# Attention block beside a gated MLP on one Trainium2 core: a planner's priorities and costs fitted anew, and one bias row spread over the partitions by GpSimd

## The chip, the core and the metric

The kernel runs on one core of a Trainium2 chip. The metric is the device time of one execution in microseconds (us): the median of three runs before the change is 158.12 us (158.08 to 158.12). Every view quoted here comes from one further execution under the hardware profiler. It took 157.98 us, of which the profile spans 156.2 us; the other 1.78 us lie outside the span. Engines are named PE (TensorE), DVE (VectorE), ACT (ScalarE), POOL (GpSimd) and SP (SyncE, which here only issues DMAs). A name with a q behind it (POOLq, SPq) is that engine's instruction queue, its sequencer.

## The reference

```python
x = A_x                                   # 1 x 2048 x 448, bf16
xn = _layernorm(x)
# A: 16 heads of 28; a token sees 8 keys, at 0, 2, ... 14 tokens back
qkv = xn @ wqkv;  kg, vg = k[idx], v[idx]
logits = einsum("bhsd,bhswd->bhsw", q, kg) * 28**-0.5   # masked where idx < 0
s = einsum("bhsw,bhswd->bhsd", softmax(logits), vg) @ wo
# B: a two-layer MLP, 448 -> 1792 -> 448
g = silu(gelu(xn @ w1 + b1) @ w2 + b2)
return x + s * g
```

## The kernel before

**The tiling.** The 2048 tokens are 16 tiles of 128 partitions, four tiles to a chunk. Even and odd tokens are laid in separate halves, so that keys 2 apart become neighbours. A tile is normalised (`stats`, `rstds`, `norm`: lines 400 to 444), turned to xnT (by PE for tiles 0 to 3, by SP's transposing DMA, L360, for the others), projected to q, k (L532) and v (L556), and q and k are turned by L360 again. The first MLP layer (`ff1`, L591, gelu on ACT at L595) goes by chunk, the second (`ff2`, L627, then y, tanh and g at L649, L655, L659) by tile.

**Attention** goes in nine visits of 228 (once 224) tokens: scores (L677, 64 matmuls), exp (ACT, L687), mask (L693, DVE or POOL), the weighted sum over v (L709, 64 matmuls), and the division through two DVE transposes (L719 to L733). POOL copies the windows of v by DMA (`move_v`, L354). `final` (L796 to L811) multiplies by wo, forms sg and o and stores the tile.

**What orders the work.** Nothing is scheduled by hand. Each piece of work is a task with an engine, a cost in us, dependencies, pool buffers and a priority. `_Plan.run` (L89) walks through time with these costs: on each engine the task that can start first goes next, and among those within `SLACK` of it the one of highest priority. The result is a fixed program order on each engine. So a cost or priority changes no operation; it changes the order on every queue.

**Pairs and hops.** Most projections and all of `ff1` have a contraction of 448 = 3 x 128 + 64. `pair` (L477) splits two such products into 64-row matmuls that run side by side on the two halves of the PE array: a first part of 8 matmuls, then a second part of 6 with the halves swapped. Between the two stands a hop: an instruction that waits for the first part and tells PE that it is done (L490). Its queue is POOL for the chunks 0 and 1 (`early`), SP or POOL later:

```python
held["told"] = (nc.gpsimd if k.on == "POOL" else nc.sync).nop()
...
told = plan.add(HOPS[0] if early else HOPS[1], 0.06, f2, [t], 300)
...
u = plan.add("PE", pe(a.n, 3), f3, [told], prio + LATER["swap"], ...)
```

**rstd on POOL.** For tiles 4 and up, 1/sqrt(var + eps) is formed on POOL in two instructions, the second waiting for the first:

```python
nc.gpsimd.tensor_scalar(sd[:, t0:t0 + n], ...)                                          # L425
nc.gpsimd.tensor_tensor(out=rstd[:, t0:t0 + n], in0=sd[...], in1=half_t, op=ALU.pow)    # L426
```

**b2** (L894) is loaded before by one DMA, issued by POOL, that reads the row of 448 numbers 128 times, once for each partition (112 KB). y (L649) and the last tile (L625) need it.

Of the kernel before, what the change touches and what calls it, by code (L numbers as in the profile page):

```python
# [164 lines left out]
def kernel(  # L165
# [12 lines left out]
    nc = tc.nc  # L178
    P = 128
    S, D, H, DH, F = A_x.shape[1], 448, 16, 28, 1792  # L180
# [9 lines left out]
    TPC = CH // P  # L190
# [26 lines left out]
    def sb(name, shape, dt=BF16):  # L217
        return const.tile(shape, dt, name=name)
# [11 lines left out]
    b2 = sb("b2", [P, D])  # L230
# [15 lines left out]
    def ring(name, n, shape, dt=BF16, fifo=False):  # L246
        return _Pool([sb(f"{name}{i}", shape, dt) for i in range(n)], fifo)
# [10 lines left out]
    p_o = ring("o", 3, [P, D])  # L258
# [9 lines left out]


    PRIO = {  # L270
        "project": (49.5, 205, 104, 52.5,),
        "project2": (147, 150, 101, 61,),
        "values": (89.5, 62.5, 21, 58,),
        "attn": (185, 179.5, 78, 174.5, 106.5, 106, 138.5, 136.5, 32.5,),
        "ff1": (185, 180, 84.5, 176.5, 66.5, 64.5, 156.5, 189.5, 203, 146, 76, 114.5, 77.5, 179.5,
            75.5, 118.5, 180.5, 14.5, 163, 68, 151, 115.5, 194.5, 167.5, 180, 188.5, 86, 93,),
        "gelu": (62.5, 22.5, 95, 92.5,),
        "ff2": (144, 162.5, 103.5, 142.5, 44.5, 112.5, 67, 5, 89, 106.5, 101.5, 75, 74, 55, 11.5,
            6.5,),
        "final": (140, 19.5, 70.5, 47, 112, 34.5, 23.5, 142.5, 73, 53, 198.5, 188.5, 81.5, 126.5,  # L280
            180, 71,),
        "norm": (37.5, 132, 179.5, 129.5, 74.5, 99, 161, 69, 63, 62, 43.5, 73, -5.5, 90, 133.5,
            150,),
        "loads": (166.5, 166, 188, 139.5, 54.5,),
        "stats": (47.5, -60, 180.5, 23, 127, 56, 188.5, 77, 197.5, -13.5, 185, 205.5, 138, 14, 52.5,
            138.5,),
        "turn_x": (108.5, -1, 28, 116, 210, 116.5, 131.5, 160, 41.5, 79.5, 70, 119, -4.5, 74.5,
            132.5, 111,),
        "turn_qk": (68.5, 112, 174.5, 90, 80, 6, 149.5, 60.5, 4, 140.5, 199.5, 96.5, 103, 166.5,
            140, 156,),  # L290
        "move_v": (81.5, 95, 23, 95, 18.5, 26.5, 8, 128, 29.5,),
        "copies": (50, 119.5, 58.5, 76, 32.5, 135.5, 43, 1, 87, 79.5, 129, 77, 32, 41.5, 135,),
    }
    LATER = {"swap": 135, "qk": 165, "v": 29.5, "gelu": 30.5, "exp": 55.5, "mask": -60, "pv": 45, "recip": -16.5, "os": 54.5, "y": 153.5, "tanh": 182.5, "g": 58, "sg": 183, "o": 120.5}

    plan = _Plan()

# [3 lines left out]
    def pe(n, k=1):  # L301
        return k * (n / 2400.0 + 0.0025)

    def act(n):
        return 0.15 + n / 1130.0
# [39 lines left out]
    def dma(eng, dst, src, kb, prio, deps=(), issue=0.5, rate=350.0):  # L345
        def fn(_):
            {"SP": nc.sync, "ACT": nc.scalar, "POOL": nc.gpsimd}[eng].dma_start(dst, src)
        a = plan.add(eng, issue, fn, [t_on] + list(deps), prio)
        return plan.add("DMA", kb / rate, lambda _: None, [a], prio, tail=1.7)
# [123 lines left out]
    def behind(later, earlier):  # L473
        tc.add_manual_dep(later.ins, earlier.ins.name,
                          mybir.DependencyInfo(mybir.DependencyClass.Sync, mybir.DependencyReason.DATA), reason="row tiles")

    def pair(a, b, prio, early=False):  # L477
# [17 lines left out]
        def f3(k):  # L495
            p, q = buf(p_b, t, 0), buf(p_b, t, 1)
            for i in together([part(b, q, kt, 0, kt + 4) for kt in range(3)], [part(a, p, kt, 1, kt + 4) for kt in range(3)])[0]:
                behind(i, held["told"])
        u = plan.add("PE", pe(a.n, 3), f3, [told], prio + LATER["swap"], tail=0.15, mode=64)
        a.evac(u, t, 0)  # L500
# [23 lines left out]
    t_row, t_qk = [[] for _ in range(NT)], {}  # L524

    def qk_rows(t, which, prio):
        cs = slice(t * P, (t + 1) * P)

        def part(ps, kt, half, start, stop):
            r = half_rows(half)  # L530
            w = w_in[r, kt, which * D:(which + 1) * D] if kt < 3 else w_in3[r, 0, :]
            return nc.tensor.matmul(ps[:, :D], xnT[r, kt, cs], w, start=start, stop=stop)  # L532

        def evac(a, own, i):
            b = qk_tok[t % len(qk_tok)]

            def fn(k):
                copy(k.on, b[:, which, :, :DH], buf(p_b, own, i)[:, :D].rearrange("p (h c) -> p h c", h=H))
            t_row[t].append(plan.add(("ACT", "DVE"), (act(D), dve(D)), fn, [a, t_qz[t % len(qk_tok)], t_qk.get(t - len(qk_tok))],
                                     prio + LATER["qk"], give=((p_b, own, i),)))  # L540
            if len(t_row[t]) == 2:
                t_qk[t] = dma_T(qkT[:, :, :, cs].rearrange("p w g c -> p (w g) c"), lambda: b[:].rearrange("p w h c -> p (w h c)"),
                                t_row[t], PRIO["turn_qk"][t], None, 2, 1.9 if t < 3 else 3.8 if t == TPC else 2.0 if t == TPC + 1 else 1.27)
        return _Job(D, part, [t_xT[t]] + t_w[0] + t_w[1] + t_w[2], evac, (), t_w[3])

    t_v, v_at, h_at = {}, {}, {}
# [3 lines left out]
    def vproj(t, prio):  # L550
# [7 lines left out]
        def evac(a, own, i):  # L558
            def fn(k):
                copy(k.on, v_tok[t][:, :, :DH], buf(p_b, own, i)[:, :D].rearrange("p (h c) -> p h c", h=H))  # L560
            t_vt[t] = plan.add(("ACT", "DVE"), (act(D), dve(D)), fn, [a] + t_vw + v_used[t], prio + LATER["v"], give=((p_b, own, i),))
        return _Job(D, part, [t_xT[t]] + t_w[0] + t_w[1] + t_w[2], evac, (), t_w[3])
# [22 lines left out]
    def ff1(c, mt, prio, gate):  # L585
# [7 lines left out]
        def evac(a, own, i):  # L593
            def fn(k):
                nc.scalar.activation(buf(p_h, own, i)[:], buf(p_b, own, i)[:], ACT.Gelu_apprx_tanh,  # L595
                                     bias=b1[:, mt:mt + 1])
            t_h[(c, mt)] = plan.add("ACT", 0.69, fn, [a, t_b1] + gate, prio + LATER["gelu"],
                                    give=((p_b, own, i),), table=("gelu",))
# [17 lines left out]
    def ff2_part(t, cs, n, end, prio):  # L616
# [30 lines left out]
        else:  # L647
            def f2(k):
                nc.vector.tensor_tensor(out=buf(p_y, k)[:, :n], in0=buf(p_b, halves[0])[:, :n], in1=b2[:, cs], op=ALU.add)  # L649
            y, pool = plan.add("DVE", dve(n), f2, [a, t_b2], prio + LATER["y"], take=(p_y,), give=((p_b, halves[0], 0),)), p_y  # L650
            held = ((p_y, y, 0),)
        after = [a, y]

        def f3(k):
            nc.scalar.activation(buf(p_t, k)[:, :n], buf(pool, y)[:, :n], ACT.Tanh, scale=0.5)  # L655
        th = plan.add("ACT", act(n), f3, after, prio + LATER["tanh"], take=(p_t,), table=("exp", "gelu"))

# [85 lines left out]
    def attn(b, what):  # L743

        deps, take, give, fns, cost = [], [], (), [], -SWITCH
        for n, (w, blk) in enumerate(what):
            if not n or what[n - 1][0] != w:
                cost += SWITCH
            cost += 0.215
            if not n:  # L750
                cost += 0.03
            at = len(take)
            if w == "S":
                fn, d = scores_of(blk)
                d = d + state["early"]
                take += [p_b] * 4
                fns.append(lambda k, fn=fn, at=at: fn([buf(p_b, k, at + i) for i in range(4)]))
            else:
                exps, masked = state[blk]
                fn, g = values_of(blk, exps)  # L760
                give += g
                d = masked + t_v[blk]
                take += [p_b] * 2
                fns.append(lambda k, fn=fn, at=at: fn([buf(p_b, k, at + i) for i in range(2)]))
            deps = deps + d + last_visit[w][-1:]

        def f1(k):
            for fn in fns:
                fn(k)
        prio = PRIO["attn"][b]  # L770
        a = plan.add("PE", cost, f1, deps, prio + (LATER["pv"] if what[0][0] == "P" else 0), take=take, give=give, tail=0.15,
                     mode=32 if what[0][0] == "S" else 33)
        a.out = 32 if what[-1][0] == "S" else 33
        at, exps = 0, []
        for w, blk in what:
            last_visit[w].append(a)
            if w == "S":
                state[blk] = weights_of(blk, a, at, PRIO["attn"][blk], state["gate"])
                exps += state[blk][0]
                at += 4  # L780
            else:
                for w in range(2):
                    output_of(blk, a, at + w, w, PRIO["attn"][blk])
                at += 2
        return exps
# [95 lines left out]
    def f_b1(k):  # L881
# [7 lines left out]
    turned = [t_xT[t].deps[0] for t in range(TPC, 2 * TPC)]  # L889
# [1 line left out]
    load_x(12, 4, 85, "SP", turned)  # L891
    t_w2 = [[dma("SP", w2[:, 7 * i:7 * i + 7, :], B_w2[F // 2 * i:F // 2 * (i + 1), :].rearrange("(m p) c -> p m c", p=P),
                 784, PRIO["loads"][4], turned, 1.0)] for i in range(2)]
    t_b2 = dma("POOL", b2[:], B_b2.rearrange("(o d) -> o d", o=1).to_broadcast((P, D)), 112, 82, turned)  # L894
    t_wo += [dma("POOL", wo[32 * g:32 * g + 28, :, :], A_wo[112 * g:112 * g + 112, :].rearrange("(l c) d -> c l d", l=4),
                 100, 80, [t_w2[1][0]] + t_wo[:1]) for g in range(G)]
    for t in range(2 * TPC, NT):
# [69 lines left out]
```

## Time and profile before

| | |
|---|---|
| median of 3 runs | 158.12 us |
| profiled execution, and its span | 157.98 us, 156.2 us |
| busy share of the span: PE, DVE, ACT, POOL | 96%, 72%, 53%, 48% |
| PE idle in the span | head 1.2 us, wait before L677 0.2 us, after the last matmul the rest |
| matmuls and weight loads | 2204 each |
| chain that ended last | PE 80%, DVE 8%, DMA 3%, POOL 2%, issue 2% |
| POOL: masks (L693), v copies (L354) | 28 (24 + 4), 52 |
| DVE: masks (L693) | 8 |

Section 1 of a page gives the busy time of each engine. Matmul ends are modelled, so a PE row that is "busy" can hide a wait; the starts of successive groups in the timeline show it. The chain of waits is followed back from the last instruction. A releaser is inferred: where it names an engine that had long been done, it was something else in the queue.

### The profile page before, as it was taken

To read this page: it belongs to the slowest core of one execution; us is meant where nothing else is said; L and a number is where in the kernel's file an instruction comes from. 1 tells how busy PE (TensorE), PEld (TensorE's weight loads), DVE (VectorE), ACT (ScalarE), POOL (GpSimd) and SP (SyncE) were. 2 spreads that over 40 slices of the span, in tenths; PEclk is the share of its full clock that TensorE was granted. 3 is DMA by queue.
4 is the path that set the end of the run, shared out by engine and by line. 5 is a ranking of instruction groups with operands and counts; after the bars stand their busy time and mean duration, and the time that the engine had idled before them with its cause. 6 is when DMAs were issued, how large, how long until landed. Compare 5 with 4: busy or idle time off the path is not lost.

```text
span 156.2 us, 5305 instructions
## 1 busy us (share of the span) xinstructions
PE 150.1 (96%) x2204; PEld 77.8 (50%) x2204; DVE 113.2 (72%) x259; ACT 83.3 (53%) x149; POOL 74.7 (48%) x123
## 2 busy tenths in 40 slices
PE   6999999999999999999999999999999999999980
PEld 2544454444455555455554644455556444545570
DVE  4789551486266758997799895109899996998992
ACT  3245867378889416444634149782496587051220
POOL 7854856000459408839261098389599780000000
PEclk9999999999999999999999999999999999999999
DMA  4999969999749443099039822123300100200211
GB/s 156 329 317 315 167 124 187 237 269 307 141 95 166 64 82 90 10 192 138 4 83 85 131 70 73 38 76 83 105 0 4 34 31 29 63 4 0 68 36 43
DMA packets 33575, 17.36 MB, mean 111 GB/s; under 512 B 25331, under 2 KB 32387, under 8 KB 33552
## 3 DMA queue, kind: packets, MB, share of 16 engines
q1 hardware_dynamic: 31472, 14.03, 41.3%
q0 software_dynamic: 1936, 2.88, 8.5%
q8 instruction: 17, 0.28, 0.8%
q10 hardware_dynamic: 144, 0.11, 0.2%
q14 instruction: 6, 0.05, 0.1%
HBM read 7.06 MB, written 1.84 MB: 57 GB/s over the span
## 4 chain that ended last, share of the span: by engine, by line
PE 80%; DVE 8%; DMA 3%; POOL 2%; issue 2%; ACT 1%; SPq 1%; DVEq 0%; ACTq 0%; POOLq 0%
PE bank L627 23%; PE bank L591 22%; PE bank L532 11%; PE bank L796 7%; PE bank L556 6%; PE bank L677 4%; PE bank L709 4%; PE bank L327 3%; DMA xnT<-xn 3%; POOL v L354 2%; DVE sg L801 2%; DVE o L807 1%; DVE w_in L659 1%; ACT E L687 1%; DVE xn L438 1%
## 5 line engine op out<-in xcount | busy, mean ns | idle before, releaser
L627 PE MATMUL bank<-w,h 128*128 128x448 bf16 (+1 forms) x238 | 45.2, 342 | 0.0
L591 PE MATMUL bank<-xnT,w 64*128 64x512 bf16 x392 | 44.7, 376 | 0.0
L595 ACT ACTIVATE h<-bank,b 128x512 bf16<-128x512 f32 x56 | 34.0, 689 | 12.9 <-PE bank L591 12.8
L354 POOL DMA_DIRECT2D v<-v_tok x52 | 27.6, 538 | 19.8 <-PE bank L709 9.0
L693 POOL TENSOR_TENSOR E<-E,m_gen 128x456 bf16<-128x456 bf16 x24 | 26.7, 1139 | 11.7 <-ACT E L687 9.5
L627 PEld LDWEIGHTS <-h 128*128 128x128 bf16 x238 | 22.3, 98 | 18.1 <-issue 0.4
L591 PEld LDWEIGHTS <-w 64*128 64x128 bf16 x392 | 19.1, 94 | 22.7 <-issue 1.1
L532 PE MATMUL bank<-w_in,xnT 64*128 64x448 bf16 (+1 forms) x212 | 24.3, 350 | 0.1
L687 ACT ACTIVATE E<-bank 128x456 bf16<-128x456 f32 (+1 forms) x36 | 17.0, 555 | 9.1 <-PE bank L677 9.1
L655 ACT ACTIVATE t<-y 128x448 f32<-128x448 f32 x15 | 8.7, 578 | 17.4 <-DVE y L649 17.4
L719 DVE STREAM_TRANSPOSE dt<-bank 128x480 f32<-128x480 f32 (+1 forms) x18 | 12.1, 671 | 5.6 <-PE bank L709 5.6
L532 PEld LDWEIGHTS <-xnT 64*128 64x128 bf16 (+1 forms) x212 | 10.6, 94 | 10.9 <-issue 1.1
L314 DVE CAST qk_tok<-bank 128x448 bf16<-128x448 f32 x16 | 9.4, 613 | 6.8 <-PE bank L532 6.8
L796 PE MATMUL bank<-wo,oT 128*128 128x448 bf16 (+1 forms) x68 | 14.1, 342 | 0.0
L312 ACT CAST qk_tok<-bank 128x448 bf16<-128x448 f32 x16 | 8.3, 533 | 10.6 <-PE bank L532 10.0
L556 PE MATMUL bank<-w_in,xnT 64*128 64x448 bf16 (+1 forms) x106 | 13.4, 349 | 0.0
L649 DVE TENSOR_TENSOR y<-bank,b 128x448 f32<-128x448 f32 x15 | 9.3, 620 | 4.9 <-PE bank L627 4.9
L728 DVE STREAM_TRANSPOSE dt<-rd 128x480 f32<-128x480 f32 (+1 forms) x18 | 12.1, 673 | 0.5
L733 DVE TENSOR_TENSOR oT<-bank,dt 128x456 bf16<-128x456 f32 (+1 forms) x18 | 11.3, 630 | 0.5
L404 DVE BATCH_NORM_STATS2 st<-x_sb 128x6 f32<-128x448 bf16 x16 | 9.6, 603 | 2.4 <-DMA x_sb<-in_A_x_dram 2.4
L438 DVE TENSOR_SCALAR xn<-x_sb,mv,rstd 128x448 bf16<-128x448 bf16 x16 | 6.3, 394 | 6.0 <-POOL rstd L426 5.8
L796 PEld LDWEIGHTS <-oT 128*128 128x128 bf16 x68 | 6.3, 98 | 6.3 <-issue 0.8
(62 smaller groups left out, 128.9 us busy)
## 6 DMA issues: line engine op xcount, KB each, us to landing
out_dram<-o SPq DMA_DIRECT2D x15, 112.0 KB, 1.7
w<-in_B_w_dram SPq DMA_DIRECT2D x2, 784.0 KB, 7.2
w<-in_B_w_dram SPq DMA_DIRECT2D x2, 672.0 KB, 7.0
x_sb<-in_A_x_dram SPq DMA_DIRECT2D x3, 448.0 KB, 6.3
v<-v_tok POOLq DMA_DIRECT2D x20, 64.0 KB, 2.5
w_in<-in_A_wqkv_dram SPq DMA_DIRECT2D x3, 336.0 KB, 4.3
w<-in_B_w_dram SPq DMA_DIRECT2D x4, 112.0 KB, 6.5
wo<-in_A_wo_dram POOLq DMA_DIRECT2D x4, 98.0 KB, 4.2
```

The lines of the kernel that those rows point to most:

```text
L354: nc.gpsimd.dma_start(dst(k), src())
L532: return nc.tensor.matmul(ps[:, :D], xnT[r, kt, cs], w, start=start, stop=stop)
L556: return nc.tensor.matmul(ps[:, :D], xnT[r, kt, k0:k0 + P], w, start=start, stop=stop)
L591: return nc.tensor.matmul(ps[:], w1[r, kt, ms], xnT[r, kt, cs], start=start, stop=stop)
L595: nc.scalar.activation(buf(p_h, own, i)[:], buf(p_b, own, i)[:], ACT.Gelu_apprx_tanh, bias=b1[:, mt:mt + 1])
L627: nc.tensor.matmul(ps[:, :n], buf(*h_at[(c, mt)])[:, j * P:(j + 1) * P], w2[:, mt, cs], start=(mt == 0 and not biased), stop=(mt == NMT - 1))
L687: nc.scalar.activation(buf(p_E, k)[:, :n], buf(p_b, a, at + hl)[:, :n], ACT.Exp, scale=SCALE)
L693: (nc.gpsimd if k.on == "POOL" else nc.vector).tensor_tensor(out=E[:, :n], in0=E[:, :n], in1=m[:, :n], op=ALU.mult)
L719: nc.vector.transpose(buf(p_dt, k)[:, :32 * m], buf(p_b, po, i)[:, :32 * m])
L728: nc.vector.transpose(buf(p_dt, d)[:, :32 * m].rearrange("p (b c) -> p b c", c=32), buf(p_rd, r)[:, :m].unsqueeze(2).to_broadcast((P, m, 32)))
L733: nc.vector.tensor_tensor(out=oT[:, :, q0:q0 + 2 * nq], in0=buf(p_b, po, i)[:, :n].rearrange("p (l q) -> p l q", l=4), in1=buf(p_dt, d)[:, ...
L796: nc.tensor.matmul(ps[:, :n], oT[:, kt, t * P:(t + 1) * P], wo[:, kt, cs], start=(kt == 0), stop=(kt == KT - 1))
```

## The change

Three things are changed, and no arithmetic:

- All priorities (`PRIO`, `LATER`) are replaced.
- Two costs of the planner are changed: an attention visit on PE from 0.215 to 0.47 us (to which the planner adds 0.095 for a switch of tiling and 0.03), and the issue of a qkT transpose on SP from 3.8, 2.0, 1.27 to 4.5, 2.2, 1.6 us for tiles 4, 5 and 6.
- b2 is loaded as one row into the last output buffer, and a new POOL instruction copies it to all partitions.

```diff
     PRIO = {
-        "project": (49.5, 205, 104, 52.5,),
+        "project": (76, 203, 109, 106.5,),
...
-    LATER = {"swap": 135, "qk": 165, "v": 29.5, "gelu": 30.5, "exp": 55.5, "mask": -60, "pv": 45, "recip": -16.5, "os": 54.5, "y": 153.5, "tanh": 182.5, "g": 58, "sg": 183, "o": 120.5}
+    LATER = {"swap": 182.5, "qk": 143.5, "v": 37.5, "gelu": 172.5, "exp": 90.5, "mask": 35, "pv": 53, "recip": 48, "os": 171, "y": 181, "tanh": 144, "g": 137, "sg": 134, "o": 74}
...
-                                t_row[t], PRIO["turn_qk"][t], None, 2, 1.9 if t < 3 else 3.8 if t == TPC else 2.0 if t == TPC + 1 else 1.27)
+                                t_row[t], PRIO["turn_qk"][t], None, 2, 1.9 if t < 3 else 4.5 if t == TPC else 2.2 if t == TPC + 1 else 1.6 if t == TPC + 2 else 1.27)
...
-            cost += 0.215
+            cost += 0.47
...
-    t_b2 = dma("POOL", b2[:], B_b2.rearrange("(o d) -> o d", o=1).to_broadcast((P, D)), 112, 82, turned)
+    b2r = p_o.bufs[-1]
+    t_b2r = dma("POOL", b2r[:1], B_b2.rearrange("(o d) -> o d", o=1), 1, 82, turned[:1])
+    t_b2 = plan.add("POOL", 0.5, lambda _: nc.gpsimd.partition_broadcast(b2[:], b2r[:1], channels=P), [t_b2r], 82)
```

The built program's order on each engine shows what the diff does not:

- The number of matmuls is the same, and so is the number of ACT table loads (6).
- On DVE there are 18 masks where there were 8, 13 o additions (L807) where there were 17, and 26 copies out of PSUM (L314) where there were 25. POOL has 18 masks where it had 28, and the other 4 o additions.
- POOL's order holds two further instructions. One, of the kind that stands at L335 ahead of the first affine_select (there the profile shows it as MODIFY_POOL_CONFIG), stands directly ahead of the new partition_broadcast and names another code library, number 1; a second stands ahead of the next L425, and names library 0 again.
- Between POOL's instructions the hops stand so (a hop is named by the number of the matmul that it waits for, counted through PE's order): 206, 214, then library 1 and the broadcast, 234, 242, 262, 270, 290, then library 0, L425, L426 (tiles 8 to 11), 298, 312, L425, L426 (tiles 12 to 15), 320, 340 and so on. Before, the order was 206, 214, 234 and so on up to 326, L425, L426, 346, L425, L426.
- PE's order in that stretch: matmuls 207 to 214 are a first part of `ff1`; 283 to 290 and 291 to 298 are first parts of v, 299 to 304 the second part that hop 290 lets go, 305 to 312 and 313 to 320 first parts of `ff1`, and 321 to 326 the second part that hop 298 lets go. Then come the rest of chunk 1's `ff1`, q and k of the tiles 8 and 9, and the first scores.
- On PE, q and k of the tiles 10 to 15 and v of the tiles 8 to 15 now stand together (84 matmuls of L532, 56 of L556). Between the first two score visits of the last chunk stand 18 matmuls of `ff2` and `final` (before: 14 of `ff2`), and the last visit's sum over v stands alone, ahead of the last 6 matmuls of `ff1`.
- On SP, four qkT transposes (before: three) stand ahead of the first xnT transpose of tile 4, and both halves of w2 are loaded ahead of the qkT transposes of tiles 4 to 7.

## The prediction

> **What bounds the kernel now.** I read the busy shares first, then PE's timeline, then the chain of waits, then what POOL's queue does around L425.
>
> ```profile
> PE 150.1 (96%) x2204; PEld 77.8 (50%) x2204; DVE 113.2 (72%) x259; ACT 83.3 (53%) x149; POOL 74.7 (48%) x123
> ```
>
> PE is the bound. Its columns in the next view are start, length, instruction, tiles, shape and count.
>
> ```profile
> 23.50 5.88 PE L532 MATMUL bank<-w_in,xnT 64*128 64x448 bf16 x56
> 29.21 13.11 PE L591 MATMUL bank<-xnT,w 64*128 64x512 bf16 x120
> 42.16 0.92 PE L556 MATMUL bank<-w_in,xnT 64*128 64x448 bf16 x8
> ...
> 61.68 5.47 PE L532 MATMUL bank<-w_in,xnT 64*128 64x448 bf16 x56
> 67.08 0.93 PE L796 MATMUL bank<-wo,oT 128*128 128x448 bf16 x4
> ...
> 114.14 0.40 PE L677 MATMUL bank<-qkT 32*64 32x57 bf16 x6
> 114.76 0.65 PE L677 MATMUL bank<-qkT 32*64 32x57 bf16 x58 [0.22 <-ACT E L687]
> 115.34 2.82 PE L627 MATMUL bank<-w,h 128*128 128x448 bf16 x14
> ...
> 150.75 0.93 PE L796 MATMUL bank<-wo,oT 128*128 128x224 bf16 x8
> ```
>
> From start to start, 120 matmuls of L591 take 42.16 - 29.21 = 12.95 us, 0.108 each; 56 of L532 take 67.08 - 61.68 = 5.40 us, 0.096 each. The same 56 take 5.71 at 23.50: 0.3 of hidden waiting, for xnT (the chain passes there from a DMA of xnT to PE at 27.31). The scores at 114.14 take 1.20 instead of the 0.63 of other visits: 0.57 of waiting. I find no other wait worth a name between 10.6 and 151.7. So an order can win only about 1 us inside PE's stretch and something in the tail, while whatever makes PE wait is lost in full. Hence the question is what PE waits for in the new order, and this leads to POOL: PE's second parts of pairs wait for hops in POOL's queue.
>
> **The change part by part.**
>
> *The order.* Counted through the built order:
> - The wait of 0.3 at 27.3: q and k of the tiles 6 and 7 are now behind 34 matmuls of `ff1` (3.7 us), so their xnT is there. But tile 4's first xnT transpose stands behind a fourth qkT transpose on SP (L360, 1.27 us) and can be up to 0.5 late. I take -0.1, between -0.3 and +0.4.
> - The wait of 0.57 at 114: between the two score visits there are now 18 matmuls of L627 and L796 (18 x 0.19 = 3.4 us) against 14 (2.75), and ACT needs 1.28 for its table and 4 x 0.47 for the exps, 3.2. I take -0.5, between -0.57 and 0.
> - The tail: the last matmul ends at 151.68, the last DVE instruction at 153.38, because DVE still divides the last visit (L723 to L733, 147.87 to 149.48) among the last finals. Now that visit's sum stands 6 matmuls of `ff1` and 28 of L627 earlier than the finals. I take -0.5, between -0.9 (DVE then only waits for PE) and 0.
> - Against this DVE has 10 more masks at 0.39, 4 fewer o additions at 0.39, one more copy at 0.61: +3.0 us on an engine that is idle 43 us. PE hides it, except in the last third, where DVE is nearly full. I take +0.2, between 0 and +1.
>
> Together -0.9 (between -1.8 and +1.4).
>
> *b2's DMA.* 112 KB fewer on queues that are not on the chain: 0.
>
> *The broadcast on POOL.* The copy itself is short: POOL's rows for one instruction on such a tile run from 0.2 (memset of 128 columns) to 1.05 (mask of 456); I take 0.5. The price is in the two instructions that the diff doesn't show, which name library 1 and then library 0. The only such instruction in the trace names library 0 at the start:
>
> ```profile
> L335 POOLq MODIFY_POOL_CONFIG  x2: 7/9/11, 0.9 to 1.0; - x2
> L335 POOL TENSOR_SCALAR_AFFINE_SELECT ident<-ident x1: 293/293/293, 1.1 to 1.1; 128x128 bf16<-128x128 bf16 x1
> ```
>
> Two writes of 9 ns, and 0.1 us later an affine_select of the ordinary 293 ns. That shows that naming a library that is there costs nothing. It does not show what fetching another costs. Bounds from rows: below, 0.13 us (0.94 to 1.07); above, a transfer of that stretch, since code has to come by DMA. The columns are transfers, KB each and us to landing; the first row is of the issues between 24 and 28 us alone, the second of the whole span.
>
> ```profile
> w<-in_B_w_dram SPq DMA_DIRECT2D x1, 784.0 KB, 8.6
> ```
>
> ```profile
> w<-in_B_w_dram SPq DMA_DIRECT2D x2, 784.0 KB, 7.2
> ```
>
> I take 8.6 for the first fetch, which starts beside that very load (27.02), and 7.2 for the second: the start row is for a library already there, the loads are rows of a stretch in which all DMA queues are full.
>
> The Trainium skill bears on this: "GPSIMD Engine Reference", section "Instruction dispatch", says that the first call to a freshly loaded POOL kernel pays about 6 us to bring its code in, with no instruction in the profile that shows it. No run here shows it yet. With 5.95 for each fetch the sum below would be 161.3 instead of 164.0; with the start row's 0.13 it would be 157.1.
>
> *When.* Matmul 214 ends at 23.50 + 44/56 x 5.71 = 28.0 now; in the new order 22 of the matmuls ahead are L591 instead of L532 (+0.3) and the wait of 0.3 is gone: 28.0. Behind it come 34 of L591 and 42 of L532/L556 up to matmul 290: 3.7 + 4.0, so 35.7. Matmuls 291 to 320 (14 and 16): 1.35 + 1.73, so PE reaches matmul 321 at 38.8 and needs hop 298 there.
>
> *Who is held.* Do hops pass while POOL works? The chain says so:
>
> ```profile
> 17.41 0.30 POOL sd L425
> ...
> 17.76 0.02 POOLq L490
> ...
> 17.80 0.73 POOL rstd L426
> ```
>
> This hop stands behind L426 in the queue, but passes at 17.76, when L425 has ended and L426 has just been handed over, not at 18.53, when L426 ends. So the queue runs ahead of the work and is held only by an instruction that itself waits: L426, for L425's result. In the new order the hops 234 to 290 are behind the broadcast, which waits for a small DMA alone, and pass. But hop 298 is behind L426, which waits for L425, which needs library 0. Before, L425 had its hops ahead of it and it was POOL that waited:
>
> ```profile
> POOL sd L425 <- PE bank L591: 14.5, 1, 14.5
> ```
>
> Sum: library 1 from 28.0 to 36.6, the broadcast to 37.1, library 0 to 44.3, L425 and its handover (0.4) to 44.7. PE has waited since 38.8: **5.9 us**. The hops 312 and 320 follow at once or 1.5 us later, when PE has 20 matmuls to do. The later chain of tiles 8 and 9 (rstd, xn, transposes) is late by as much as PE, so it adds nothing. Without the fetches L425 would run when the seventh statistic is there (some 37.5 by DVE's rows: loads landed at 31, 0.73 a tile, two copies) and hop 298 would be 0.9 ahead of PE.
>
> *PE's clock.* After the idle start the warm-up matmuls of 512 columns come one in 0.43 us, twice the 0.216 of a full pair later:
>
> ```profile
> 3.78 0.15 PEld L327 LDWEIGHTS <-h 128*128 128x128 bf16 x1 [0.28 <-issue]
> 4.21 0.15 PEld L327 LDWEIGHTS <-h 128*128 128x128 bf16 x1 [0.28 <-issue]
> ```
>
> This lasts from 1.25 to 5.06, 3.8 us at half rate, a loss of 1.9. Whether an idle stretch of 6 us brings it back is not in this trace: between 0 and 1.9, I take the middle, 1.0. The Trainium skill ("TensorE: Matmul & The Clock Gate", section "The HAM clock gate") has the clock halved after about 3.4 us of idleness and restored after as long of work; by that it would be 1.7, and the total 0.7 more.
>
> **Sum** on the profiled execution: 157.98 - 0.9 + 5.9 + 1.0 = 164.0 us. The median of the runs is 158.12, 0.14 above it; I leave that inside the rounding: **164.0 us**.
>
> **Rivals.**
>
> *The queue itself stands still while a library is fetched* (18%). For: the profile shows no such fetch, so my evidence on hops is of ordinary instructions only. Against: the two writes at the start ran while a memset was still at work. Then hop 234 comes at 36.6, while PE needs it 28 matmuls behind 214, at 31.0: 5.6; the second switch is reached at 41.3 and lets hop 298 go at 48.9, needed at 44.4: 4.5. With the clock twice: 157.98 - 0.9 + 10.1 + 2.0 = 169.2 us.
>
> *The way back is short, or no code is fetched at all* (16%): faster. Place: hop 298. It decides where the second switch takes less than 38.8 - 35.7 - 0.4 = 2.7 us; the first is hidden up to 7.2 in any case. For: the row at L335. Then only the order is left: 157.98 - 0.9 = 157.1 us. The change then does what it says.
>
> *The order alone goes wrong* (4%): the seventh statistic, the first xnT of tile 4, or a mask on the fuller DVE comes late, fetches cost nothing, 158.5 to 160.
>
> **How the numbers follow.** Forecast 62%: with fetches of 5 us each PE waits 2.3, with 8.6 each 7.3 and 1.9 of clock, with the order's bounds 159 to 168. The range must reach to the first rival and leaves out the faster one (16%) and the edges: 159 to 171 us. A measurement of this kernel can tell about 0.2%, 0.3 us, from no change. Faster 0.13 (most of the second rival), same 0.02, slower 0.85.
>
> **What would show it.** Right: after, two gaps of several us on POOL, one ahead of the broadcast and one ahead of the L425 at 36 to 45 us; PE with a wait ahead of the L556 group of 6 (matmul 321), released by POOL's queue; hops 234 to 290 on time. The stall at 114 gone, the DVE end closer to PE's. Wrong: PE dense from 28 to 45 us (no fetch, or a short one), or a first wait already ahead of the L591 group at 31 us (the queue stands still), or L425 late for want of statistics.

## The result, and the profile after

The changed kernel takes 170.06 us (median of four runs, 168.46 to 170.53), the kernel before 158.1 beside it: ratio 1.0746, interval 1.0671 to 1.082. It is slower by 7.5%. The profiled execution is the shortest of the four: 168.46 us, span 166.7, so 10.5 us of span more than before. In the changed kernel every line behind the table `PRIO` is one lower, up to the load of b2 (L555 is before's L556, L424 and L425 are before's L425 and L426, the hop is L489); the new broadcast is L895. The page's second part, a digit for each fortieth of the span:

```profile
PE   7999989994199999989989998999999899999990
PEclk9999999999569999999999999999999999999998
```

Before, PE's row was nines from the second slice to the 38th. A slice is now 4.17 us. PE falls to 4 and 1 tenths in the slices 10 and 11 (37.5 to 45.8 us), and the granted clock (PEclk) is down to 5 and 6 tenths in the slices 11 and 12. PE's timeline (start, length, instruction, count, idle time ahead and its releaser) says where the rest lies:

```profile
24.02 0.93 PE L531 MATMUL bank<-w_in,xnT 64*128 64x448 bf16 x8 [0.53 <-DMA xnT<-xn]
...
37.46 1.89 PE L590 MATMUL bank<-xnT,w 64*128 64x512 bf16 x16
45.26 1.30 PE L555 MATMUL bank<-w_in,xnT 64*128 64x448 bf16 x6 [5.91 <-POOLq L489]
46.35 7.30 PE L590 MATMUL bank<-xnT,w 64*128 64x512 bf16 x54
53.49 2.81 PE L531 MATMUL bank<-w_in,xnT 64*128 64x448 bf16 x28
...
71.60 2.81 PE L626 MATMUL bank<-w,h 128*128 128x448 bf16 x14 [0.62 <-DVE y L648]
...
84.96 4.70 PE L555 MATMUL bank<-w_in,xnT 64*128 64x448 bf16 x47 [0.44 <-DVE qk_tok L313]
...
104.42 0.93 PE L795 MATMUL bank<-wo,oT 128*128 128x448 bf16 x4 [0.96 <-DVE oT L732]
```

I measure a loss from start to start: the time to the next group's start, less the count times the rate at which the same matmuls go undisturbed (0.108 us for L590, 0.096 for the 64-row ones, 0.187 for L626). It comes out a little larger than the idle time in brackets (6.1 against 5.91 us ahead of L555). For the changed kernel's profiled execution this gives:

| where PE loses | us |
|---|---|
| ahead of L555, hop 298 | 6.1 |
| the 60 matmuls behind it, at the lower clock | 1.8 |
| tile 4's xnT, at 24 (before: 0.3 for xnT at 27) | 0.9 |
| VectorE late: y at 71, qk_tok at 79 and 85, oT at 104, sg and y at 132, the visit at 147 (before: none) | 0.7 + 0.4 + 0.7 + 1.1 + 0.8 + 0.4 = 4.1 |
| scores near 114 (before: 0.6) | 0 |
| last matmul to the end of the span: 3.9 (before 4.5) | -0.6 |

With before's own 0.3 and 0.6 taken off, that is 6.1 + 1.8 + 0.6 + 4.1 - 0.6 - 0.6 = 11.4; the remaining -0.9 lies in differences under 0.5 us each, some -0.3 of it in the first 16 us.

What held PE is told by POOL's rows (instruction, count, duration in ns, first and last start) for the two fetches, and by the chain of waits in order of time:

```profile
L895 POOLq MODIFY_POOL_CONFIG  x2: 16/16/16, 28.8 to 28.9; - x2
L895 POOL PARTITION_BROADCAST b<-o x1: 518/518/518, 37.3 to 37.3; - x1
```

```profile
L424 POOLq MODIFY_POOL_CONFIG  x2: 120/120/120, 37.8 to 37.8; - x2
```

```profile
38.53 6.32 issue
44.85 0.30 POOL sd L424
...
45.19 0.03 POOLq L489
...
45.26 1.30 PE bank L555 x6
```

The reader is to see a POOL that does nothing from 28.9 to 37.3 and from 37.9 to 44.85, with no instruction in the gaps. The hop passes when L424 ends, and PE starts 0.07 us later. During the first gap PE's timeline has no wait at all: the hops 234 to 290 passed. I call such a gap a fetch, after the instruction that names another library. What fills it the profile doesn't show: it has no instruction there, and in the kernel with the broadcast alone (below) no DMA traffic is recorded in the second gap (0 GB/s).

### The profile page after: what moved, and what is told of

Its sections match the earlier page's. It is cut to its first block, busy times and chain, and to the rows that moved or that the text cites. A ratio compares the mean times of both kernels' runs of the same rounds, so it can differ in the third digit from the quotient of the medians.

```text
span 166.7 us, 5308 instructions
## 1 busy us (share of the span) xinstructions
PE 152.0 (91%) x2204; PEld 79.0 (47%) x2204; DVE 118.0 (71%) x266; ACT 83.0 (50%) x148; POOL 68.4 (41%) x118
## 4 chain that ended last, share of the span: by engine, by line
PE 60%; DVE 19%; DMA 9%; issue 7%; SPq 2%; POOL 1%; ACT 1%; DVEq 0%; POOLq 0%; ACTq 0%
PE bank L626 19%; PE bank L590 17%; PE bank L531 8%; PE bank L795 6%; PE bank L555 5%; DMA x_sb<-in_A_x_dram 5%; DMA v<-v_tok 4%; DVE st L403 3%; PE bank L708 2%; DVE w_in L658 2%; PE bank L676 2%; DVE sg L800 2%; DVE y L648 2%; SPq L359 1%; DVE qk_tok L313 1%
## 5 line engine op out<-in xcount | busy, mean ns | idle before, releaser
L590 PE MATMUL bank<-xnT,w 64*128 64x512 bf16 x392 | 46.2, 384 | 0.0
L626 PE MATMUL bank<-w,h 128*128 128x448 bf16 (+1 forms) x238 | 45.4, 342 | 0.6 <-DVE y L648 0.6
L626 PEld LDWEIGHTS <-h 128*128 128x128 bf16 x238 | 22.4, 98 | 19.4 <-issue 1.8
L590 PEld LDWEIGHTS <-w 64*128 64x128 bf16 x392 | 19.6, 96 | 23.5 <-issue 3.1
L531 PE MATMUL bank<-w_in,xnT 64*128 64x448 bf16 (+1 forms) x212 | 24.7, 350 | 0.9 <-DMA xnT<-xn 0.5
L692 POOL TENSOR_TENSOR E<-E,m_gen 128x456 bf16<-128x456 bf16 x15 | 16.3, 1102 | 12.3 <-ACT E L686 10.5
L555 PE MATMUL bank<-w_in,xnT 64*128 64x448 bf16 (+1 forms) x106 | 13.6, 362 | 6.4 <-POOLq L489 5.9
L531 PEld LDWEIGHTS <-xnT 64*128 64x128 bf16 (+1 forms) x212 | 11.2, 94 | 11.4 <-issue 1.1
L437 DVE TENSOR_SCALAR xn<-x_sb,mv,rstd 128x448 bf16<-128x448 bf16 x16 | 6.3, 394 | 14.5 <-POOL rstd L425 10.7
L732 DVE TENSOR_TENSOR oT<-bank,dt 128x456 bf16<-128x456 f32 (+1 forms) x18 | 11.4, 632 | 0.6
L555 PEld LDWEIGHTS <-xnT 64*128 64x128 bf16 (+1 forms) x106 | 6.2, 96 | 11.7 <-POOLq L489 6.4
L311 ACT CAST v_tok<-bank 128x448 bf16<-128x448 f32 x8 | 4.3, 536 | 14.3 <-PE bank L555 14.2
```

What stands on the lines that cost most here:

```text
L311: nc.scalar.copy(o, i)
L555: return nc.tensor.matmul(ps[:, :D], xnT[r, kt, k0:k0 + P], w, start=start, stop=stop)
L590: return nc.tensor.matmul(ps[:], w1[r, kt, ms], xnT[r, kt, cs], start=start, stop=stop)
L626: nc.tensor.matmul(ps[:, :n], buf(*h_at[(c, mt)])[:, j * P:(j + 1) * P], w2[:, mt, cs], start=(mt == 0 and not biased), stop=(mt == NMT - 1))
L692: (nc.gpsimd if k.on == "POOL" else nc.vector).tensor_tensor(out=E[:, :n], in0=E[:, :n], in1=m[:, :n], op=ALU.mult)
```

## The experiments

My theory behind the result: two library fetches make rstd of tiles 8 to 11 late, PE stands still for it and loses clock, and besides that the new order is worse by itself. The rivals: the order's losses are only an echo of the stall; a fetch costs by itself, wherever it stands; the slow matmuls behind the stall are slow for another reason; the hop alone is what holds PE. Ratios are to the kernel before on the same chip. Every kernel computes the whole reference.

**The order without the broadcast.** The changed kernel's order, b2 by before's DMA:

```diff
-    t_b2r = dma("POOL", b2r[:1], B_b2.rearrange("(o d) -> o d", o=1), 1, 82, turned[:1])
-    t_b2 = plan.add("POOL", 0.5, lambda _: nc.gpsimd.partition_broadcast(b2[:], b2r[:1], channels=P), [t_b2r], 82)
+    t_b2r = dma("POOL", b2[:], B_b2.rearrange("(o d) -> o d", o=1).to_broadcast((P, D)), 1, 82, turned[:1])
+    t_b2 = plan.add("POOL", 0.5, None, [t_b2r], 82)
```

> The changed kernel's order on every engine, but b2 comes as before by a DMA that repeats the row 128 times, and GpSimd broadcasts nothing and fetches no library. Theory A (mine since the changed kernel's trace): the fetches cost 6.1 us of PE waiting before L555 and about 1.8 us of clock after it, and the rest of the loss is the order's own, so this kernel ends at 160 to 162 us, with the late steps at L590 (tile 4), L676, L555 and L795 still in its trace. Theory B (what the prediction said of the order, -0.9 us): these late steps are only the stall's echo, and this kernel ends at about 157.1 us. Both: PE dense from 30 to 53 us, granted clock full there.

161.41 us (160.42 to 162.48), ratio 1.0234 (1.0197 to 1.0272). The order alone costs 3.7 us. The late steps are all still in its PE timeline, so they are no echo of the stall. The wait for tile 4's xnT is 1.9 us in the profiled run, which is the longest of the six.

**The broadcast without the order.** Before's order on the other four engines, with the row load and the broadcast:

```diff
-    t_b2 = dma("POOL", b2[:], B_b2.rearrange("(o d) -> o d", o=1).to_broadcast((P, D)), 112, 82, turned)
+    b2r = p_o.bufs[-1]
+    t_b2r = dma("POOL", b2r[:1], B_b2.rearrange("(o d) -> o d", o=1), 1, 82, turned)
+    t_b2 = plan.add("POOL", 0.5, lambda _: nc.gpsimd.partition_broadcast(b2[:], b2r[:1], channels=P), [t_b2r], 82)
```

> The kernel before with its own order on PE, DVE, ACT and SyncE; b2 is loaded as one row and spread by GpSimd's broadcast, which falls in POOL's queue behind the moves of v and ahead of the four-tile pair of L425/L426 (before's lines). Theory A: two fetches (about 8.5 and 7 us) hold that pair, a hop behind it holds PE for some 5 us, and the clock after it costs 1 to 2 us: 163 to 165.5 us. Theory B (the stall is peculiar to the new order, where the hops stand behind the pair): the time stays at 158 to 159 us, though the gaps on POOL are there.

167.29 us, ratio 1.061 (1.0587 to 1.0632), above what I had expected. The waits of PE name one cause:

```profile
PE bank L591 <- POOLq L490: 7.4, 1, 7.4
```

The hop, in POOL's queue, holds a second part of six L591 matmuls. By starts the wait loses 7.5 us and the clock 2.1 behind it. I had misjudged when the first fetch begins: in this order it stands behind hop 290, and the queue reaches it only at 36.5. It takes 5.9 us, the way back 7.1, and L425 comes at 50.1.

**One POOL instruction moved.** In the changed kernel, the broadcast goes behind the second four-tile pair:

```diff
             nc.gpsimd.tensor_tensor(out=rstd[:, t0:t0 + n], in0=sd[:, t0:t0 + n], in1=half_t[:, :n], op=ALU.pow)
+            if t0 == 12:
+                nc.gpsimd.partition_broadcast(b2[:], p_o.bufs[-1][:1], channels=P)
...
-    t_b2 = plan.add("POOL", 0.5, lambda _: nc.gpsimd.partition_broadcast(b2[:], b2r[:1], channels=P), [t_b2r], 82)
+    t_b2 = plan.add("POOL", 0.5, lambda _: None, [t_b2r], 82)
```

> The changed kernel, orders unchanged on PE, DVE, ACT and SyncE; on POOL alone the broadcast is issued after the second four-tile pair of L424/L425 instead of ahead of the first, so that no pair waits for a library. Theory A (the way back to the first library, ahead of L424, is what costs): no wait of PE at L555 near 39 us, and the time is that of the order-alone kernel within 0.5 us, although the broadcast and its fetch are there. Theory B (the fetch costs by itself, by what it takes from DMA queues or by POOL standing still): a PE wait of over 2 us stays somewhere between 30 and 60 us, and the time is over 2 us above the order-alone kernel's.

162.02 us, ratio 1.028 (1.0257 to 1.0303), 8 us under the changed kernel and 0.6 over the order alone. Both fetches are still made. The first, from 41.2 to 46.9 us, holds nobody. The way back now stands ahead of the first mask on POOL (L694): that mask starts at 69.1, where the order alone has it at 62.6. In the profiled execution, at 164.0 the longest of the six, the late masks share the time from 72 to 77 us with VectorE's g, which takes 2.87 us there instead of 0.62, and PE waits twice:

```profile
76.74 0.93 PE L557 MATMUL bank<-w_in,xnT 64*128 64x448 bf16 x8 [0.79 <-DVE sg L802]
78.99 6.38 PE L557 MATMUL bank<-w_in,xnT 64*128 64x448 bf16 x47 [1.32 <-DVE qk_tok L313]
```

Behind them the clock is granted at half from 79.1 to 82.6 us, which costs another 1.8 us. The order alone has only the second of them, with 0.44, and besides a wait for y of 0.64 that is missing here. So the way back is not free in this order; whether it is the 0.6 us of the medians was not isolated. The 8 us belong to the place of the broadcast.

**The same on before's order** (the two edits together):

> The kernel before with its own order on PE, DVE, ACT and SyncE; b2 is loaded as one row (112 KB of DMA fewer) and spread by GpSimd, but the broadcast stands behind both four-tile pairs of L425/L426 instead of ahead of them. Theory A (the spread costs only what its place makes wait): no PE wait beyond those of the kernel before, 157.7 to 158.4 us, against 167.3 us with the broadcast ahead of the pairs. Theory B (the 112 KB saved are worth something): under 157.5 us. Theory C (the fetch costs by itself): over 159 us.

157.85 us against 158.09, ratio 0.9998 (0.9977 to 1.0019). Here the spread by GpSimd costs nothing that can be measured, although both fetches are made (43.9 to 49.6 us, and 55.4 to 62.3 ahead of a mask), and the 112 KB of DMA that it saves bring nothing that can be measured. The six figures side by side:

| us (ratio) | no broadcast | behind the pairs | ahead of the pairs |
|---|---|---|---|
| before's order | 158.1 | 157.85 (0.9998) | 167.29 (1.061) |
| the new order | 161.41 (1.0234) | 162.02 (1.028) | 170.06 (1.0746) |

**PE kept busy in the gap.** 28 matmuls with weights of zero, ahead of hop 298:

```diff
             held["last"] = together([part(a, p, kt, 0, kt) for kt in range(4)], [part(b, q, kt, 1, kt) for kt in range(4)])[-1]
+            if warm:
+                for _ in range(28):
+                    held["last"] = (held["last"][0], nc.tensor.matmul(q[:, :D], row0[64:128, :], w_in[64:128, 0, 2 * D:], start=False, stop=False))
...
```

(`warm` is set for the value pair of tiles 6 and 7.)

> The changed kernel with 28 more matmuls (64 rows of zeros by w_in, 448 columns, added into the bank of the value pair of tiles 6 and 7, so that nothing is changed in what it holds) ahead of the wait, some 5.2 us of work in a time in which PE had stood still. Theory A (the loss after the wait is the clock, and the clock falls because PE stood still): the granted clock stays full at 45 to 53 us, the 54 matmuls of L590 behind the wait take 5.8 us instead of 7.1, and the time falls by 1.5 to 1.9 us against the changed kernel, to 166.6 to 168.4 us. Theory B (the matmuls behind the wait were slow for another reason, such as DMA or late operands): the time stays at 168.4 to 170.5 us or rises.

168.48 us (167.08 to 169.17), ratio 1.0674 (1.0627 to 1.0722): the time alone doesn't tell the theories apart. PE's timeline does (here L558 is L555, L593 is L590, L534 is L531):

```profile
47.50 0.74 PE L558 MATMUL bank<-w_in,xnT 64*128 64x448 bf16 x6 [1.92 <-POOLq L492]
48.08 5.99 PE L593 MATMUL bank<-xnT,w 64*128 64x512 bf16 x54
54.16 2.82 PE L534 MATMUL bank<-w_in,xnT 64*128 64x448 bf16 x28
```

The same 60 matmuls take 54.16 - 47.50 = 6.66 us, against 53.49 - 45.26 = 8.23 in the changed kernel and 6.39 in the order alone. With PE busy the clock stays full, and the slowness goes. The windows views say so, with the granted clock third from the right, of the changed kernel and then of this one:

```profile
45.20:53.50 8.30, 8.24 (x62) 3.41 (x64) 3.34 (x12) 4.67 (x8) 5.21 (x8) 0.77 0.48 73
```

```profile
45.40:54.20 8.80, 6.79 (x63) 2.88 (x64) 2.56 (x9) 4.96 (x9) 5.50 (x9) 1.00 0.32 67
```

The gain of 1.6 us was mostly given back ahead of it: this run's first fetch began 1.0 us later and took 9.3 us, the second 7.45, so the hop passed 2.2 us later.

**The hops out of POOL's queue.** The eight hops behind the first four-tile pair (298 to 396) into ACT's:

```diff
+                if t0 == 8:
+                    spare["left"] = 8
                 nc.gpsimd.tensor_scalar(sd[:, t0:t0 + n], ...)
...
-            held["told"] = (nc.gpsimd if k.on == "POOL" else nc.sync).nop()
+            if 0 < spare["left"] and k.on == "POOL":
+                spare["left"] -= 1
+                held["told"] = nc.scalar.nop()
+            else:
+                held["told"] = (nc.gpsimd if k.on == "POOL" else nc.sync).nop()
```

> The changed kernel, both library fetches as they are; the eight hops that stand behind the first four-tile pair of L424/L425 in POOL's queue (those for matmuls 298 to 396) are put into ACT's queue instead, and nothing else is moved. Theory A (what stops PE is the hop held behind the pair, and what is late next is tile 8's xnT, since rstd still comes at about 45.7): no wait of PE near 39 us; a new wait ahead of L531 at about 45.6 us, until xn (0.6 us) and its transpose (some 1.3 us to issue, as much to land) have followed rstd, so 2 to 3 us in place of 5.9, and 0.5 to 1.5 us of clock after it: 164 to 166.5 us. Theory B (PE waits for the fetch or for rstd whatever queue the hops are in): the wait stays near 39 us with 5 to 6 us, and the time is 168.5 to 170 us.

169.16 us (168.44 to 170.34), ratio 1.0692 (1.0657 to 1.0726). Each theory was half right. There is no wait near 39 us, so the hop was what held PE there; but the time hardly falls. PE's timeline, then DVE's (L597 is L590, L440 is L437, L428 is L425):

```profile
40.79 3.83 PE L597 MATMUL bank<-xnT,w 64*128 64x512 bf16 x34
50.35 4.45 PE L597 MATMUL bank<-xnT,w 64*128 64x512 bf16 x20 [5.73 <-DVE v_tok L313]
```

```profile
47.60 0.40 DVE L440 TENSOR_SCALAR xn<-x_sb,mv,rstd 128x448 bf16<-128x448 bf16 x1 [8.22 <-POOL rstd L428]
...
49.68 0.62 DVE L313 CAST v_tok<-bank 128x448 bf16<-128x448 f32 x1
```

The same wait, 5.7 us, has moved 5 us on. VectorE's queue has xn of tiles 8 to 11, which waits for rstd, and behind it the copy of a v tile, which frees the bank that PE wants next (a bank is a buffer that PE fills and another engine must copy out before PE can use it again).

**The hops and that copy moved.** As above, and:

```diff
-                copy(k.on, v_tok[t][:, :, :DH], ...)
+                copy("ACT" if t == 7 else k.on, v_tok[t][:, :, :DH], ...)
```

> The kernel with the eight hops in ACT's queue (169.2 us), and besides tile 7's cast of v, which frees a bank and stood in VectorE's queue behind the normalizing of tiles 8 to 11 (L440, which waits for rstd), given to ScalarE. Theory A (rstd reaches PE by three ways, one behind another: the hop, the cast, tile 8's xnT): the wait of 5.7 us for v_tok goes, and PE waits ahead of L538 for tile 8's xnT instead, from about 47 to 51 us, some 3.5 to 4.5 us; with less lost on the clock 167 to 168.5 us. Theory B (the cast was the last of it): no wait over 1 us between 39 and 55 us, 161.5 to 163 us.

170.07 us (168.43 to 170.75), ratio 1.0751 (1.0706 to 1.0795). PE runs on to 47.3 us and waits there (L538 is L531):

```profile
53.20 5.26 PE L538 MATMUL bank<-w_in,xnT 64*128 64x448 bf16 x28 [5.89 <-DMA xnT<-xn]
```

That is theory A's third way, with 5.9 us instead of 3.5 to 4.5: xn is ready at 48.2, and the transposes of the first tiles need until 53.2. rstd reaches PE by three ways, and each makes it wait some 6 us once those ahead of it are gone. So the loss is set by when rstd comes. The clock costs 2.5 us behind this wait (28 matmuls in 5.19 us instead of 2.7).

**The fourth transpose put back.** The order alone, but SyncE issues the fourth qkT transpose (tile 3) behind the xnT transposes of tiles 4 to 7, as before:

```diff
         def fn(_):
+            if keep:
+                kept.append(lambda: nc.sync.dma_start_transpose(out=dst, in_=src()))
+                return
             nc.sync.dma_start_transpose(out=dst, in_=src())
+            if then and kept:
+                passed.append(1)
+                if len(passed) == 4:
+                    kept.pop()()
...
```

(`keep` is set for the qkT of tile 3, `then` for every xnT.)

> The order-alone kernel (161.4 us), with one transfer put back where the kernel before has it: SyncE issues the fourth transpose of qkT behind the four transposes of tiles 4 to 7's xnT instead of ahead of them. Theory A (tile 4's xnT is late because that transpose, some 2.9 us of SyncE's queue, stands ahead of it): the PE wait for xnT (0.5 to 1.9 us in the runs so far, 0.7 to 2.0 us of lost time) goes, and the median falls to 159.8 to 160.7 us. Theory B (xnT is late because xn or rstd is): the wait stays, and the time is 161.4 us.

160.41 us (160.06 to 161.02), ratio 1.0161 (1.0136 to 1.0187), 0.7% under the order alone, and the wait is gone from PE's list. SyncE's queue in the changed kernel, then in the kernel before:

```profile
11.82 8.49 SPq L359 DMA_TRANSPOSE qkT<-qk_tok  x4
20.39 5.15 SPq L359 DMA_TRANSPOSE xnT<-xn  x4
```

```profile
11.92 5.68 SPq L360 DMA_TRANSPOSE qkT<-qk_tok  x3
```

The fourth makes 8.49 - 5.68 = 2.8 us more of the queue; its own record is 2.50 us (17.80 to 20.30), not 1.27.

**Copies off VectorE.** The order alone, with the qk copies of tiles 8 to 15 all on ACT:

```diff
-                copy(k.on, b[:, which, :, :DH], ...)
+                copy("ACT" if t >= 2 * TPC else k.on, b[:, which, :, :DH], ...)
```

> The order-alone kernel (161.4 us), with the eight casts of tiles 8 to 15's qk rows that VectorE does given to ScalarE in the same places of the order (some 4.4 us off VectorE, 4.4 us onto ScalarE, which is busy 1.6 to 1.8 us in 6 there). Theory A (PE's waits for qk_tok at 73 and 79 us, 0.43 and 0.68 us of lost time, come from a VectorE that has no gap between 62 and 80 us): both waits go, and the time falls by 0.8 to 1.3 us, to 160.1 to 160.6 us; the waits for y, oT and sg stay. Theory B (VectorE's fullness there is not what holds PE): 161.4 us.

161.18 us (160.01 to 163.8), ratio 1.019 (1.0153 to 1.0227). Both waits for qk_tok are gone from the trace, and the waits for y (0.6), oT (0.6) and y (0.3) stay, as theory A has it. But the time lies between the two theories, and the interval overlaps that of the order alone, so it shows no clear gain. In the profiled execution 0.5 us comes back in losses of 0.3 at a score visit near 53 and 0.2 near 82.

**Both edits together:**

> The order-alone kernel with both edits: the fourth qkT transpose behind tiles 4 to 7's xnT, and the eight qk casts of tiles 8 to 15 on ScalarE. If both theories A hold and add: 158.8 to 159.8 us, with the waits for y (0.7 us), oT (0.8 us) and sg, y near 125 us (0.8 us) still in the trace, which is why it would still not be below the kernel before (157.7 us in the runs of this chip). If one only removes what the other uncovers: 160 to 160.6 us.

160.25 us (159.34 to 161.43), ratio 1.0152 (1.0114 to 1.019): no more than the transpose alone gave. The 1.1 us of the two waits go, but 0.5 come back as above, and 0.4 at 46 us, where PE now waits for an xnT.

**Masks off VectorE too.** Both edits, and the eighth visit's masks on GpSimd:

```diff
-                (nc.gpsimd if k.on == "POOL" else nc.vector).tensor_tensor(out=E[:, :n], ...)
+                (nc.gpsimd if k.on == "POOL" or b == 7 else nc.vector).tensor_tensor(out=E[:, :n], ...)
```

> The kernel with both edits (fourth qkT transpose behind xnT, eight qk casts on ScalarE; 160.25 us) and the three masks of the eighth visit that VectorE does at 120 to 122 us given to GpSimd, which stands idle there from 120 to 125 us. Theory A (the waits for sg and y at 123 and 124 us, 0.39 us each, come from a full VectorE): both go, 159.4 to 159.9 us. Theory B (they come from the order of VectorE's own chain): 160.2 us, or more if GpSimd's masks, some 1.05 us each, come too late for the visit that reads them.

160.12 us, ratio 1.014 (1.0107 to 1.0172): the time of theory B. The losses for sg and y near 124 us stay at 0.4 each. With the masks gone, y comes 0.3 us earlier against the matmuls around it, but VectorE waits 0.7 us for ACT's t, and its g takes 0.95 us beside the masks on GpSimd, where it took 0.63 with GpSimd idle. That gives the 0.3 us back. So this run doesn't decide between a full VectorE and the order of its chain.

**A table loaded early.** Before's order with the broadcast behind the pairs, and a tiny Exp behind the third chunk's last Gelu:

```diff
                 nc.scalar.activation(buf(p_h, own, i)[:], buf(p_b, own, i)[:], ACT.Gelu_apprx_tanh,
                                      bias=b1[:, mt:mt + 1])
+                done[c] = done.get(c, 0) + 1
+                if c == 2 and done[c] == NMT:
+                    nc.scalar.activation(early[:], eps_t[:], ACT.Exp)
...
```

> The kernel before's own order, with b2 as one row and GpSimd's broadcast behind both four-tile pairs of L425/L426 (157.85 us), and one more instruction on ScalarE: an Exp of 128x1 elements right behind the last Gelu of the third chunk, so that the activation table (1.28 us) is loaded in the 5 us in which ScalarE stands idle there (106.5 to 111.5), and not when the scores of the visit at 111 us arrive. Theory A (the 0.56 us that PE loses at L677 near 114 us, the one wait left between 30 and 150 us, is that load): the wait goes, and the time falls by 0.4 to 0.6 us, to 157.2 to 157.5 us, below both kernels. Theory B (another engine is late there too, or VectorE's work behind it sets the end): within 0.2 us of 157.85.

157.47 us against 157.72, ratio 0.997 (0.9949 to 0.9992): by 0.3% below the kernel before, and so below both kernels; the interval excludes no change narrowly. ACT's timeline, then PE's (L602 is the new line, L693 is before's L687, L683 before's L677):

```profile
107.04 1.28 ACT L602 ACT_TABLE_LOAD   x1
108.33 0.20 ACT L602 ACTIVATE early<-eps_t 128x1 f32<-128x1 f32 x1
112.05 0.55 ACT L693 ACTIVATE E<-bank 128x456 bf16<-128x456 f32 x1 [3.51 <-PE bank L683]
```

```profile
114.65 0.70 PE L683 MATMUL bank<-qkT 32*64 32x57 bf16 x64
```

The load has moved into the idle time, and the 64 matmuls that took 1.20 us before take 0.63 by starts.

## Why the prediction held, and where it did not

The number was 164.0 in a range of 159 to 171; the time is 170.06. The main step, PE held at hop 298 by the two fetches, held in mechanism and size. The order was wrong in sign, and so the sum came out 4.5 us short of the profiled execution. That the time lies in the range is partly luck: the forecast's own bounds were 159 to 168 (158.5 to 168.6 by its terms), and the range goes on to 171 only for the rival of a queue that stands still, which fell.

- **"Whatever makes PE wait is lost in full."** Right: every wait of the table above is in the time.
- **The broadcast and b2's DMA** (0.5 and 0): 0.52 measured, and 157.85 against 158.09 with the DMA saved.
- **Fetches of 8.6 and 7.2 us**: 8.5 and 7.0. That both came so close is luck, since the two numbers were the times of weight loads, and no run ties a fetch to them; with the broadcast elsewhere the first took 5.7 to 5.9. The reason given for the second, that the DMA queues were full, is not right: it took 7.1 us in the kernel with the broadcast alone, where no DMA traffic is recorded beside it (0 GB/s). The Trainium skill's 5.95 us ("GPSIMD Engine Reference", "Instruction dispatch") is near the first fetch beside 84 to 197 GB/s of DMA traffic (5.7 to 5.9) and short of both here.
- **"PE has waited since 38.8: 5.9 us"**: PE's idle time is 5.91 us, and it is hop 298. The queue ran ahead as argued from before's chain, so the rival of a queue that stands still (169.2) fell, though its number lies closer to the time. So did the rival without a fetch.
- **"The later chain of tiles 8 and 9 is late by as much as PE, so it adds nothing."** It adds nothing, but it is no lesser holder: with the hop out of the way it costs the same 6 us. I had named one holder where there are three.
- **The clock, 1.0 (0 to 1.9)**: 1.8, and the kernel with PE kept busy shows that it is the clock. The Trainium skill ("TensorE: Matmul & The Clock Gate", "The HAM clock gate") gave an estimate of 1.7, from one window of some 3.4 us, and agrees here; behind the other waits the loss was 2.1 to 2.9, more than one window makes. In the changed kernel and the three with these other waits the granted clock is at half for 6.8 us (42.2 to 49.0 in the changed one), and the loss is half of what is left of that when PE starts again: 3.8 us here, 4.1 to 5.8 in the others.
- **The order, -0.9 (-1.8 to +1.4)**: failed. By itself it costs 3.7 us. Of its four terms, the stall at 114 (-0.5, measured -0.6) came as said. *The tail* (-0.5) came by the mechanism, but half as large: VectorE ends 1.46 us behind PE instead of 1.70, in every kernel with the new order, so 0.24 us. The rest of the table's -0.6 lies between VectorE's last instruction and the end of the span, 2.5 to 2.8 us in either order. *Tile 4's xnT* (-0.1, at most +0.4) was mis-sized: I charged the fourth transpose at 1.27 us, the price of one that waits for nothing, where before's own row of three in 5.68 us says 1.9; it took 2.5 and cost about 1.1 us (0.7% of the time). *The fuller VectorE* (+0.2, at most +1) measured 4.1 us: I set 3 us more against 43 us of idle time in the whole span. What counts is the stretch: in the order alone VectorE is busy 5.83, 5.90 and 5.45 us of each 6 from 62 to 80 us, because, as I read the timelines, the 84 and 56 matmuls of projection that now stand together ask for their copies while three visits are divided. The experiments show it for the two waits for qk_tok; for the others only the trace speaks, and the run with the masks moved doesn't decide it near 124. With both edits the order still costs 1.5%, and that rest is not traced to a cause by any run. The windows view of the order alone (us, busy time of PE, PEld, DVE, ACT and POOL, clock, DMA):

```profile
62.00:68.00 6.00, 5.36 (x151) 3.20 (x149) 5.83 (x10) 2.76 (x6) 4.89 (x8) 1.00 0.16 43
68.00:74.00 6.00, 5.83 (x54) 2.76 (x53) 5.90 (x12) 1.79 (x4) 3.25 (x3) 1.00 0.00 0
74.00:80.00 6.00, 5.56 (x60) 3.36 (x58) 5.45 (x8) 1.60 (x3) 1.03 (x1) 1.00 0.69 131
```

  ACT, with 1.6 to 2.8 of 6 us, had room for the copies; the reader is to look at DVE and ACT side by side.
- **Sum**: 157.98 + 5.9 (6.1) + 1.0 (1.8) - 0.9 (+2.6) gives 164.0 (168.5, the profiled execution). The median lies 1.6 above that: the profiled execution was the shortest, and the times of the new order spread over some 2 us. Why they spread is open. The xnT wait varies between profiled executions (0.5 to 1.9 us), but two of the three kernels without it at tile 4 spread over 2.0 and 2.1 us too.

## What to carry to other kernels

Here an instruction that changes GpSimd's code library took some 6 to 9 us for the way there and some 7 for the way back, and what that cost was decided by what waited behind it on that queue: list the users of the next ordinary POOL instruction, and put the switch where they are all served. When one wait is found, ask what the same late value holds on the other queues before pricing its removal. Price a fuller engine by the stretch in which it has no gap, not by its idle time over the span.

## What the runs showed of the hardware

- The first fetch took 5.7 to 5.9 us beside 84 to 101 GB/s of DMA traffic, 5.9 beside 197, and 8.1 to 9.3 beside 262 to 314. The four long ones also stand at the same place of the program, so traffic is not shown as the cause. The way back to L424 took 7.0 to 7.5 beside 0 to 75. During the first the queue's later hops pass.
- Behind a PE wait of 5.9 us the granted clock was 0.52 for as long as 5.2 us (the kernel with hops and copy moved, from 53.2 on). Two waits of 0.8 and 1.3 us within 3.1 us were followed by 3.4 us at half (one POOL instruction moved, from 79.1 on).
- VectorE's instructions stretch beside POOL's: where POOL masks and adds near 118 us, a mask on VectorE takes 1.22 us instead of 0.39, and near 122 us a g takes 0.95 with three masks moved to POOL and 0.63 without them. This was seen, not isolated.
